# Pooled attention and a max-out feed-forward layer on one core: output weight loaded in two halves, first weight product moved to the prologue, every step reordered

## The chip, the cores and the metric

The kernel runs on one core of a Trainium2 chip. The metric is the device time of one launch in microseconds (us). Three runs of the kernel before gave a median of 227.07 us (225.73 to 227.32). Times inside an execution are counted from the start of the profiled span. For this kernel a difference under about 1% of the time is treated as no change.

## What is computed

For 8 batches of 8 heads, 576 positions and 64 channels, keys and values are averaged over groups of 8 positions, queries attend to the 72 averaged keys, and the result (4608 tokens by 512) passes through three weights, an element-wise maximum and an output weight:

```python
k_p = k.reshape(B, H, Sp, 8, D).mean(axis=3); v_p = v.reshape(B, H, Sp, 8, D).mean(axis=3)
attn = softmax(q @ k_p.T / sqrt(D)); x = (attn @ v_p) as 4608 x 512
h = np.maximum(np.maximum(x @ w1, x @ w2), x @ w3)        # w1..w3: 512 x 768
out = h @ w_out                                           # w_out: 768 x 512
```

## The kernel before, in words

**The work.** The kernel uses the identity h = w1-part + max(0, x(w2-w1), x(w3-w1)). `sub_w` (L392) subtracts w1 from w2 and w3 in place on DVE; `turn_w` (L399) transposes w1, and `linear` (L405) multiplies it with the output weight into `wm` (512x512), 24 matmuls of 512 columns. `hidden` (L439) makes the two products and the maximum for a block of 512 tokens; `project` (L459) adds x times `wm` and h times `w_out` for four groups of 128 tokens. There are nine blocks (0 to 8) of tokens and eight batches (0 to 7) of attention. Blocks 1 to 5 use `out_seven` (L699) for the projection, and blocks 6 to 8 use `seven` (L810) for the hidden part: seven block products in place of eight, with sums of operands prepared on DVE or POOL.

**One batch of attention.** Loads of q, k and v go through POOL's DMA queue and convert float32 to 16 bits (L73, L82, L94). Keys and values are summed over 8 positions by three additions (`fold_steps`, L157) on POOL; only the keys of batches 0 and 1 are summed on DVE (0 with PE), and the values of batch 0 on PE. Queries are turned by PE in batches 0 to 2 (`turn_q`, L188) and by a DMA transpose that SP issues from batch 3 on (step `T`, L350). `scores` (L239) multiplies, ACT takes the exponential, `values` (L301) multiplies with the folded values, DVE normalises, and `turn_x` (L284) turns the result into `xT`: by PE up to batch 2, by SP's DMA transposes after that.

**The order.** Nothing is reordered by a scheduler: every engine does its instructions in the order in which the program names them. Four lists hold it. The prologue (L530 to L571) is written as calls. `block(0, {...})` (L870) runs hidden and project of block 0 with steps of batches 0 and 1 at numbered slots. `MIDDLE` (L953) lists blocks 1 to 5, `ORDER` (L906) the rest. A name such as `2:s0-` is a step of batch 2 (q: turn queries, k: turn keys, K: fold keys on DVE, s: scores, v: values, x: turn the result, T: transpose queries by DMA), `1/h` a hidden product of block 1, `1/6` an output product, `1/b2` a sum of operands, `k3+4` four steps of a fold on POOL, `q4<` a load. A trailing `-` issues PE's part and parks the eviction, `+` issues the oldest parked eviction.

**Queues.** The loads at the start are POOL instructions, in the order L112, L120, L127 to L136: q0 (two DMAs), v0 (two), nine parts of w1, w2, w3 (columns 0-255 of each, then 256-511, then 512-767), the whole of w_out, then k1, q1, v1, q2, k2, v2. Each takes one of eight semaphores, so a ninth DMA waits until the DMA eight before it has landed. k0 comes through SP. SP also issues the stores of the output and the DMA transposes, in program order. A load marked `<` waits for the last hidden matmul issued before it and for the last query transpose (L886 to L891).

**PSUM.** The prologue has a pool `ps0` (three tiles `att` of two banks, two tiles `one`). It is closed at L568, and a pool `psp` (two `att`, one `tr`, three `pw`) serves to the end of `MIDDLE`, a third (`psq`) after it.

Of the kernel before, what the change touches and what calls it, by code (L numbers as in the profile page):

```python
# [10 lines left out]
ALU = mybir.AluOpType  # L11


@with_exitstack
def kernel(
# [18 lines left out]
    C = H * D  # L34
# [17 lines left out]
    ld = ctx.enter_context(tc.tile_pool(name="ld", bufs=2))  # L52
    sb2 = ctx.enter_context(tc.tile_pool(name="sb2", bufs=2))
    sb3 = ctx.enter_context(tc.tile_pool(name="sb3", bufs=3))
# [3 lines left out]
    first = ExitStack()  # L58
    stage.enter_context(first)
    pools = [first.enter_context(tc.tile_pool(name="ps0", bufs=1, space=PSUM))]  # L60
# [21 lines left out]
    def load_v(b, eng, dtype=F16, cuts=(0, H)):  # L82
        if b == 0:
            vts[0] = ld.tile([96, 4096], dtype, name="vt0", tag="vt")[:, 0:3072].rearrange(
                "p (h i d) -> p h i d", h=H, i=6)
            src = v[0].rearrange("h (p i) d -> p h i d", i=6)
            return [eng.dma_start(out=vts[0][:, h:g], in_=src[:, h:g])
                    for h, g in zip(cuts, cuts[1:])][-1]
        vts[b] = ld.tile([Sp, H, POOL, D], dtype, name="vt", tag="vt")
        src = v[b].rearrange("h (sp j) d -> sp h j d", j=POOL)  # L90
        return [eng.dma_start(out=vts[b][:, h:g], in_=src[:, h:g])
                for h, g in zip(cuts, cuts[1:])][-1]
# [13 lines left out]
    def load_w(part):  # L106
        for t, wap in zip(w_sb, (moe_w1, moe_w2, moe_w3)):
            nc.gpsimd.dma_start(  # L108
                out=t[:, :, part],
                in_=wap.rearrange("(kc p) j -> p kc j", p=128)[:, :, part])  # L110
# [9 lines left out]
    load_v(0, nc.gpsimd, cuts=(0, 4, 8))  # L120
    pick = const.tile([96, 6, 128], F16, name="pick", tag="pick")
    nc.gpsimd.memset(pick, 1.0)
    for sign in (1, -1):
        nc.gpsimd.affine_select(
            out=pick, in_=pick, compare_op=ALU.is_ge, fill=0.0, base=7 * (sign < 0),
            pattern=[[sign, 6], [-8 * sign, 128]], channel_multiplier=6 * sign)
    for i in range(3):  # L127
        load_w(slice(256 * i, 256 * i + 256))
    nc.gpsimd.dma_start(
        out=wo_sb, in_=moe_w_out.rearrange("(jc p) c -> p jc c", p=128))  # L130
    load_k(1, nc.gpsimd, F16)
    load_q(1)
    load_v(1, nc.gpsimd)
    load_q(2)
    load_k(2, nc.gpsimd)
    load_v(2, nc.gpsimd)  # L136
# [72 lines left out]
    def turn_k(b):  # L209
        pkt = keys(b, PW if b in KP else SC if len(pools) == 3 else ATT)  # L210
# [13 lines left out]
    def score(b, h, out, tp, i0, i1):  # L224
# [3 lines left out]
        rows = slice(64 * (f % 2), 64 * (f % 2) + 64) if len(pools) == 2 else slice(0, 128)  # L228
# [72 lines left out]
    def values(b, c0):  # L301
        tag = (ATT0, ATT, ("val", 1))[len(pools) - 1]
# [21 lines left out]
    ATT0, ONE = ("att", 3), ("one", 2)  # L324
# [16 lines left out]
    def do(b, steps):  # L341
# [3 lines left out]
        for name in steps.split():  # L345
# [12 lines left out]
            elif name[0] == "s":  # L358
                if i == 0 and name[-1] != "+":
                    new_et(b)  # L360
                if len(pools) == 3:
# [18 lines left out]
            elif name[0] == "w":  # L380
                turn_w(i, nc.scalar.copy if i % 2 else nc.vector.tensor_copy)
# [17 lines left out]
    def turn_w(jc, evac):  # L399
        pwt = psum([128, KCH, 128], F16, name="pwt", tag=TR[0], bufs=TR[1])  # L400
# [4 lines left out]
    def linear():  # L405

        for kc in range(KCH):
            pm = psum([128, C], F32, name="pm", tag="pw", bufs=3)
            for jc in range(JCH):
                nc.tensor.matmul(pm, w1T[:, jc, bass.ts(kc, 128)], wo_sb[:, jc, :],  # L410
                                 start=(jc == 0), stop=(jc == JCH - 1))
                if jc == JCH // 2 - 1:
                    yield
            (nc.scalar.copy if kc % 2 else nc.vector.tensor_copy)(
                out=wm_sb[:, kc, :], in_=pm)
            yield
# [22 lines left out]
    def hidden(n):  # L439
# [13 lines left out]
        if n == 0:  # L453
            yield from linear()
# [4 lines left out]
    def project(n):  # L459
        hT = hTs[n]  # L460
        for mm in range(4):
# [5 lines left out]
            for c in ((slice(0, C // 2), slice(C // 2, C)) if last else (slice(0, C),)):  # L467
                tag = PW if len(pools) < 3 else PA if last else PO
# [20 lines left out]
    wm = psum([128, 1024], F32, name="wm", tag="att", bufs=3)[:, 0:512]  # L489
# [9 lines left out]
    def new_pk0():  # L499
        pk0.append(psum([D, 3, 96], F32, name="pk0", tag=ONE[0], bufs=ONE[1]))  # L500
# [16 lines left out]
    def scores4(h):  # L517
        psc = psum([128, 4, 256], F32, name="psc4", tag="att", bufs=3)
# [4 lines left out]
    def scores2(h):  # L523
        psc = psum([128, 2, 512], F32, name="psc2", tag="att", bufs=3)
# [5 lines left out]
    heat(10)  # L530
    add_k0(0, 2)
    new_pk0()
    sum_k0(0, 0)
    sum_k0(0, 1)
    heat(3)
    add_k0(2, 2)
    new_pk0()
    sum_k0(0, 2)
    sum_k0(1, 3)
    for par in range(2):  # L540
        put_k0(0, par, nc.scalar.copy)
    heat(2)
    add_k0(4, 2)
    sum_k0(1, 4)
    sum_k0(1, 5)
    for par in range(2):
        put_k0(1, par, nc.vector.tensor_copy)
    turn_q(0, 0, 5, nc.vector.tensor_copy, ATT0)
    turn_q(0, 5, 9, nc.scalar.copy, ATT0)
    heat(2)  # L550
    scores4(0)
    turn_q(0, 9, 14, nc.vector.tensor_copy, ATT0)
    turn_q(0, 14, 18, nc.vector.tensor_copy, ATT0)
    pool_v(0, 0, 4, ONE, nc.vector.tensor_copy)
    scores4(4)
    pool_v(0, 4, 8, ONE, nc.vector.tensor_copy)
    scores2(0)
    values(0, CHUNKS[0][0])()
    scores2(2)
    values(0, CHUNKS[1][0])()  # L560
    turn_x(0, 0, 0, xns[0, 0], ONE)
    scores2(4)
    sub_w(0, 0, 1, (1,))
    turn_x(0, 128, 0, xns[0, 128], ONE, nc.vector.tensor_copy)
    sub_w(0, 0, 1, (2,))
    sub_w(0, 1, 2)
    scores2(6)
    first.close()  # L568
    pools.append(stage.enter_context(tc.tile_pool(name="psp", bufs=1, space=PSUM,
                                                  reuse_waits="tile")))  # L570
    turn_w(0, nc.scalar.copy)  # L571

    def block(n, plan, stages):

        for slot, end in enumerate(part for stage in stages for part in stage(n)):
            if end:
                end()
            for b, steps in plan.get(slot, ()):  # L580
                if b < B:
                    do(b, steps)
# [116 lines left out]
    def out_seven(n):  # L699
# [21 lines left out]
        def bank(of, m):  # L721
            if n < LAST:
                if of not in banks:
                    if mid:
                        tag = (TR if of == "A" else PW) if len(pools) < 3 else {
# [84 lines left out]
    def seven(n):  # L810
# [41 lines left out]
        def evict(i, g, p):  # L852
# [11 lines left out]
            elif i in (5, 7) and (12 - i, g) in done:  # L864
# [4 lines left out]
    fold_v(1)  # L869
    block(0, {0: [(0, "v2")], 1: [(0, "v3")], 3: [(0, "x2 x3 w1 v4")], 6: [(0, "x4 d1")], 9: [(0, "w2")], 10: [(0, "d2")], 11: [(0, "w3")], 12: [(0, "w4")], 14: [(0, "w5 z")],  # L870
              15: [(0, "S S")], 17: [(1, "K")], 18: [(0, "S S")], 24: [(1, "q0 k")], 25: [(1, "q1")],
              26: [(1, "s0 q2")], 28: [(1, "s3 Q3")], 30: [(1, "s6")], 31: [(1, "v0")],
              32: [(1, "v1 x0")], 33: [(1, "X1 v2 v3")]}, (hidden, project))
    load_k(3, nc.gpsimd)
    load_v(3, nc.gpsimd)
    load_q(3)
    fold_k(2, nc.gpsimd)
    fold_v(2)


# [178 lines left out]
```

## Time and profile before

The profiled execution has a span of 224.5 us; the median of the timed runs is 227.07 us, 2.6 us more, which lies around the span.

| what | value |
|---|---|
| median of 3 runs (lowest, highest) | 227.07 us (225.73, 227.32) |
| span of the profiled execution | 224.5 us |
| PE busy | 213.0 us, 95%, 1884 matmuls |
| DVE, ACT, POOL busy | 157.9, 123.2, 140.9 us |
| share of the chain that ended last: PE, DMA, POOL, DVE | 69%, 12%, 8%, 6% |
| first matmul; end of the last | 1.53 us; about 220.7 us |

The page gives each engine's busy time. PE is busy nearly throughout, so the question at each stage is how much of PE's time goes to waits, to filler (`heat`, L491) or to a slow start. The view of windows gives busy time per stretch; the timeline of one engine gives its instructions in order, each with the idle time before it and who ended it.

### The profile page before, as it was taken

The numbers are of one execution on the slowest core, as the hardware profiler recorded it, in microseconds if no ns is written. First come the engines' busy times: TensorE is split into PE (matmuls) and PEld (weight loads), VectorE is DVE, ScalarE is ACT, GpSimd is POOL, SyncE is SP. The second block draws the span as 40 slices with busy tenths as digits, with TensorE's granted clock in tenths as the row PEclk, the third lists the DMA queues.
The fourth block names the chain that finished last, engine by engine and source line by source line (L and its number), as shares of the span: only waits on it lengthen the run. The fifth ranks groups of instructions, "written<-read, shape, count | busy, mean of one in ns | idle before, by whom it ended". The sixth has DMA issues, their size and how long they took to land.

```text
span 224.5 us, 4870 instructions
## 1 busy us (share of the span) xinstructions
PE 213.0 (95%) x1884; PEld 147.3 (66%) x1885; DVE 157.9 (70%) x308; ACT 123.2 (55%) x239; POOL 140.9 (63%) x121
## 2 busy tenths in 40 slices
PE   7788999999999999999999999999799999999993
PEld 2477744458659744964685478447589667788882
DVE  3658989037998795885679468629767977878940
ACT  2267524846784577266735845493694445564330
POOL 7974300999957969787685669794292903881020
PEclk9999999999999999999999999999999999999999
DMA  6999999989749799739987998599420645200265
GB/s 167 212 197 196 207 208 207 204 170 226 135 106 190 131 177 248 124 58 212 252 93 157 227 217 140 75 257 157 103 56 19 167 100 110 47 0 3 65 198 161
DMA packets 47303, 33.55 MB, mean 149 GB/s; under 512 B 26992, under 2 KB 42288, under 8 KB 47280
## 3 DMA queue, kind: packets, MB, share of 16 engines
q0 software_dynamic: 16944, 16.98, 47.2%
q1 hardware_dynamic: 29888, 15.87, 31.2%
q10 hardware_dynamic: 448, 0.39, 0.7%
q8 instruction: 15, 0.25, 0.4%
q14 instruction: 8, 0.07, 0.1%
HBM read 34.60 MB, written 9.44 MB: 196 GB/s over the span
## 4 chain that ended last, share of the span: by engine, by line
PE 69%; DMA 12%; POOL 8%; DVE 6%; ACT 2%; issue 1%; POOLq 0%; DVEq 0%; ACTq 0%
PE pw L423 22%; PE oA L769 13%; DMA vt<-in_v_dram 8%; PE oC L769 7%; PE pA L846 6%; DMA mw<-in_moe_w_dram 4%; PE pav L305 4%; PE oB L769 3%; PE psc L229 3%; PE po L475 3%; PE pC L846 3%; POOL half L163 2%; PE po L471 2%; DVE xn L315 1%; POOL mw L108 1%
## 5 line engine op out<-in xcount | busy, mean ns | idle before, releaser
L423 PE MATMUL pw<-xT,mw 128*128 128x512 f16 (+1 forms) x336 | 68.4, 349 | 0.2 <-ACT xT L299 0.2
L423 PEld LDWEIGHTS <-mw 128*128 128x128 f16 x336 | 30.7, 98 | 26.3 <-issue 1.8
L163 POOL TENSOR_TENSOR half<-vt 72x1024 f32<-72x1024 f16 (+1 forms) x12 | 29.1, 2443 | 20.5 <-DMA vt<-in_v_dram 13.2
L431 DVE TENSOR_TENSOR hT<-t,pw 128x512 f16<-128x512 f16 (+1 forms) x42 | 25.4, 608 | 21.4 <-PE pw L423 12.1
L234 ACT ACTIVATE et<-psc 72x512 f16<-72x512 f32 (+2 forms) x66 | 33.9, 571 | 9.0 <-PE psc L229 8.9
L165 POOL TENSOR_TENSOR half<-half 72x1024 f32<-72x1024 f32 (+1 forms) x13 | 28.1, 2165 | 10.4 <-DVE rcp L313 5.2
L429 ACT ACTIVATE t<-pw 128x512 f16<-128x512 f32 (+1 forms) x42 | 22.6, 538 | 17.0 <-PE pw L423 16.5
L315 DVE TENSOR_TENSOR xn<-pav,rcp 128x512 f16<-128x512 f32 x40 | 27.7, 691 | 1.4
L163 POOL TENSOR_TENSOR half<-ktFalse 96x768 f32<-96x768 f16 (+1 forms) x11 | 19.3, 1767 | 3.9 <-issue 3.8
L855 ACT CAST pad<-pA 128x512 f16<-128x512 f32 x27 | 15.1, 586 | 11.6 <-PE pA L846 9.1
L780 ACT COPY osb<-oA 128x512 f32<-128x512 f32 x20 | 11.8, 588 | 17.4 <-PE oA L769 17.2
L769 PEld LDWEIGHTS <-tt 128*128 128x128 f16 x200 | 18.9, 98 | 2.4
L229 PEld LDWEIGHTS <-kz 64*128 64x128 bf16 (+1 forms) x161 | 8.8, 95 | 12.4 <-issue 8.0
L305 PE MATMUL pav<-vp,et 72*128 72x65 f16 x320 | 16.4, 194 | 0.6 <-DVE xn L315 0.2
L305 PEld LDWEIGHTS <-et 72*128 72x128 f16 x320 | 15.0, 98 | 3.0 <-issue 1.3
L313 DVE RECIPROCAL rcp<-pav 128x8 f32<-128x8 f32 x40 | 8.1, 202 | 10.9 <-PE pav L305 10.8
L846 PEld LDWEIGHTS <-sw 128*128 128x128 f16 x144 | 13.8, 97 | 2.7 <-issue 0.2
L826 DVE SCALAR_TENSOR_TENSOR hT<-pad 128x512 f16<-128x512 f16 x18 | 14.0, 784 | 1.1 <-ACT pad L859 0.5
L823 DVE TENSOR_TENSOR pad<-pad,pC 128x512 f16<-128x512 f16 x18 | 12.3, 682 | 3.5 <-PE pC L846 2.7
L229 PE MATMUL psc<-qT,kz 64*128 64x256 bf16 (+5 forms) x138 | 13.2, 263 | 1.0 <-DVE qT L197 0.9
L620 POOL TENSOR_TENSOR pad<-xT 128x256 f16<-128x256 f16 x8 | 5.5, 689 | 13.0 <-DMA xT<-xn 13.0
L769 PEld LDWEIGHTS <-hT 128*128 128x128 f16 x126 | 12.3, 98 | 1.4
(122 smaller groups left out, 400.6 us busy)
## 6 DMA issues: line engine op xcount, KB each, us to landing
out_dram<-osb SPq DMA_DIRECT2D x32, 128.0 KB, 4.3
ktFalse<-in_k_dram POOLq DMA_DIRECT2D x7, 576.0 KB, 8.0
qb<-in_q_dram POOLq DMA_DIRECT2D x7, 576.0 KB, 7.7
vt<-in_v_dram POOLq DMA_DIRECT2D x7, 576.0 KB, 11.9
out_dram<-osb SPq DMA_DIRECT2D x11, 256.0 KB, 6.7
mw<-in_moe_w_dram POOLq DMA_DIRECT2D x9, 256.0 KB, 9.4
ktTrue<-in_k_dram SPq DMA_DIRECT2D x3, 384.0 KB, 5.4
out_dram<-ob SPq DMA_DIRECT2D x8, 128.0 KB, 2.8
```

The lines of the kernel that those rows point to most:

```text
L163: yield e.tensor_tensor(out=f[:, at], in0=t[:, at, 0:4, :], in1=t[:, at, 4:8, :], op=ALU.add)
L165: yield e.tensor_tensor(out=f[:, :, 0:2, :], in0=f[:, :, 0:2, :], in1=f[:, :, 2:4, :], op=ALU.add)
L229: nc.tensor.matmul(out, kz_all[b % 2][f % 2][rows, h, :], qTs[b][rows, n + i0:n + i1, 64 * (h % 2):64 * (h % 2) + 64], start=True, stop=True)
L234: nc.scalar.activation(out=out, in_=in_, func=FT.Exp, scale=1.0 / 64.0)
L305: nc.tensor.matmul(pav[:, h // 4, 65 * (h % 4):65 * (h % 4) + 65], ets[b][:, h, c0:c0 + 128], vp_all[:, b, h, :], start=True, stop=True)
L315: nc.vector.tensor_tensor(out=xn, in0=pv[:, :, :, 0:D], in1=rcp.to_broadcast([128, 2, 4, D]), op=ALU.mult)
L423: mm = nc.tensor.matmul(pw, w_sb[wi][:, kc, bass.ts(jc, 128)], x[:, kc], start=(kc == 0), stop=(kc == KCH - 1))
L429: yield lambda t=t, pw=pw: nc.scalar.activation(out=t, in_=pw, func=FT.Relu)
L431: yield lambda t=t, pw=pw: nc.vector.tensor_tensor(out=hT[:, jc, c0:c1], in0=t, in1=pw, op=ALU.max)
L769: nc.tensor.matmul(p, left, right, stop=(r == 4), skip_group_check=True, start=(i in FIRST and r == 0 and (m == 0 or n == LAST)))
L846: mm = nc.tensor.matmul(p[:, w], a[:, kc, bass.ts(g, 128)], b[:, kc, :], start=(i in FIRST and w + kc == 0), stop=(w + kc == 2), skip_grou ...
L855: nc.scalar.copy(out=kept(i, g), in_=p)
```

## The change

1. Tiles of the SBUF pools `ld`, `sb2`, `sb3` are taken from a class `Ring` that numbers the buffers in turn; the same number of buffers.
2. One PSUM pool `psp` serves the prologue, block 0 and `MIDDLE`: in the prologue two `att` tiles, one `tr`, three `pw` (before: three `att`, two `one`).
3. The order of the first loads is a list. w_out is loaded as two DMAs of 256 columns each (`o0`, `o1`; the weights' parts are `w10` for w1, part 0, and so on; `v1 v0` are heads 4-7 and 0-3 of batch 0; `pick` is POOL's own work of making a constant). q1 is loaded ahead of k1.
4. `linear` becomes four pieces of 12 matmuls with 256 columns (rows half i, columns half c), and with all six `turn_w` is named in the prologue.
5. Prologue and block 0 are names in `MIDDLE` (a leading `.` for the prologue, `0/h` and `0/p` for block 0's hidden and project). The folds of values 1, keys 2 and values 2 on POOL are single steps in the list.
6. Loads marked `<<` (k3, v3, q3) wait for no matmul. All of `MIDDLE` and `ORDER` is in a new order with the same steps.

```diff
-    ld = ctx.enter_context(tc.tile_pool(name="ld", bufs=2))
+    ld = Ring(ctx.enter_context(tc.tile_pool(name="ld", bufs=1)), 2)
...
-    pools = [first.enter_context(tc.tile_pool(name="ps0", bufs=1, space=PSUM))]
+    pools = [Ring(stage.enter_context(tc.tile_pool(name="psp", bufs=1, space=PSUM,
+                                              reuse_waits="tile")))]
...
+    LOADS = """
+        w10 v1 v0 w11 pick w12 w20 o0 w30 w21 o1 w22 w31 w32 Q1 K1 V1 K2 V2 Q2
+    """
...
+    def linear(i, c, tag, evac):
+        pm = psum([128, 2, C // 2], F32, name="pm", tag=tag[0], bufs=tag[1])
+        part = slice(C // 2 * c, C // 2 * c + C // 2)
+        for m in range(2):
             for jc in range(JCH):
-                nc.tensor.matmul(pm, w1T[:, jc, bass.ts(kc, 128)], wo_sb[:, jc, :],
+                nc.tensor.matmul(pm[:, m], w1T[:, jc, bass.ts(2 * i + m, 128)], wo_sb[:, jc, part],
                                  start=(jc == 0), stop=(jc == JCH - 1))
...
+        evac(out=wm_sb[:, 2 * i:2 * i + 2, part], in_=pm)
...
     ORDER = """
-        b1 o1- 2a- b3 o1+ k7- b2 1a- 1b- v62- 1a+ k7+ 2a+ b4 T o6- s70- o6+ o2- s70+ o2+ 6a-
+        k7- o1- 2a- 1a- v62- b1 b3 o1+ 1b- b2 1a+ o6- k7+ s70- o2- s71- 2a+ T vpool 6a- o6+ s70+
...
     MIDDLE = """
-        1/h- q4< k4< 1/h+ 1:x2 1:v4- 1/h- 1/h- v4< 1/h+ 1:v4+ 1/h+ 1/h- 1:x3 1/h- 1/h+ 1/h+
+        .h10 .a0 .n .m0 .a1 .n .m1 .h3 .m3 .a2 .m2 .h2 .ka .m4 .m5 .q0 .kb .Q1 .s0 .h2 .Q2 .s2 .T0
+        .Q3 k3<< .S0 .S4 .v4 .v0 .V0 .T3 .s4 .T5 .T4 .T2 .s6 .V1 .T1 0:v2- .e001 .x0 .X1 .l10 0/h
+        .l00 .e011 0:v3- .e012 0:v2+ .e002 0/h- 0:v3+ 0/h- 0/h+ 0/h+ 0:z .L11 0:x2 0:x3 0:d1 .l01
+        0/h- v1+1 0:v4- 0/h- 0/h+ 0/h- 0/h- 0/h- 0/h+ S 0/h- 0/h- 0/h+ 0/h+ S 0/h+ 0/h- 0/h+ 0:v4+
+        1:q0 0/h+ 0/h+ v1+1 0/h- 0/h- 0:d2 1:q2 0/h+ 0/h+ 0/h- 1:K 0/h+ v1+1 0/h- 0:x4 0/h- 0/h+
+        1:q1 S v1+1 1:k- k2+2 0/h- 0/h+ 0/h+ 0/h- 1:k+ v3<< 0/p 1:s0- 1:s0+ q3<< 0/h+ 1:s0+ 1:s0+
+        k2+1 1:s0+ S 0/p 0/p 1:s3- 1:s3+ 1:s3+ 1:Q3 S 1:s3+ 1:s3+ 0/p 1:s6- 1:s6+ 1:s6+ 0/p 1:v0
+        1:v1 0/p 1:v2- k2+1 v2+1 1:x0 v2+1 S 0/p S 1:X1 0/p 1:v3- 1:v2+ 1/h- 1:v4- 1/h+ 1:x2 1/h-
...
-        4/h+ 4/h- 4/b1 4/h+ 4/h ! k6+2 5:s6- 5:s6+ 4/h 4/h 4/b3 4/b2 4/b4 5:s6+ ! k6+2 4/1-
+        4/7- 5:x0 4/1+ 4/2+ 5:v2- 5:v1+ v6+1 5:x1 v6+1 4/6- 5:v2+ 6:T 4/7+ 5:v3- 6:k- q7< 5:v4-
+        4/6+ 5:x2 4/5- 4/b4 5:v3+ 4/5+ 5/h- 6:k+ 4/3- 4/4- 6:s0- 5:v4+ v7< 5/h- 5/h+ 5/a1 6:s0+
...
-        5/h+ 6:s3- 5/h+ 7:T 6:s3+ 5/h- 6:s3+ 5/h- 6:s3+ 6:s3+ 5/h+ 6:s6- 5/h+ 6:s6+ 6:s6+ 5/h
-        5/h- 6:v0 5/h+ 5/h- 6:x0 6:v1- 5/h+ 6:v1+ 6:x1
+        6:v0- 6:v1- 5/h+ 5/h- 6:v0+ 6:x0 6:v1+ 7:T 5/h+ k7+1 4/3+ 5/h+ 5/h- 5/h- 5/h+ 5/h+ 6:x1
+        k7+1
     """
```

In the prologue's names, `h10` is ten filler matmuls, `a` and `m` the sum of batch 0's keys, `q0 Q1 Q2 Q3` the turning of its queries (through the single tile `tr`), `s` and `S` scores, `v4 v0` the folding of its values by PE, `V` values, `T0` to `T5` the six `turn_w` (`T4 T5` need `w12`, `T2 T3` need `w11`), `l10 l00 L11 l01` the four pieces of `linear` (the second digit is the half of w_out), `e` and `0:d` the subtractions.

More of the change, by code (lines that the diff above doesn't have):

```diff
@@ L119 @@
     make_identity(nc, identh)
[L120 to L136, printed above, removed]
+    loads()
     kz_all = [[const.tile([128, H, 128], BF16, name=f"kz{i}{par}", tag=f"kz{i}{par}")
@@ L550 @@
[L550 to L582, printed above, removed]
+    TAGS = {"q": TR, "t": PW, "l": PW, "v": PW, "x": PW}
@@ L867, in seven @@
         return product
[L869 to L878, printed above, removed]
     folding = {}
@@ L986, in middle @@
                     pieces[n] = hidden(n)
-                parts(name, lambda: next(pieces[n]))
+                parts(name, lambda: next(pieces[n]) or (lambda: None))
+            elif n == 0 and step == "p":
+                if not pieces.get("p"):
+                    pieces["p"] = project(0)
+                next(pieces["p"])
             elif step == "f":
```

224 lines of the change are left out of this document (133 added, 91 removed).

## The prediction

> **What bounds the kernel now.** I read the page's busy times and its 40 slices, then the windows by stage, then PE's and POOL's timelines where PE is not full, and last the query transposes on SP.
>
> ```profile
> PE 213.0 (95%) x1884; PEld 147.3 (66%) x1885; DVE 157.9 (70%) x308; ACT 123.2 (55%) x239; POOL 140.9 (63%) x121
> PE   7788999999999999999999999999799999999993
> DMA  6999999989749799739987998599420645200265
> ```
>
> PE is the bound from about 20 us to 220 us; the loads fill the DMA queue for the first nine slices. So a change of order can gain only where PE waits. The windows say where.
>
> ```profile
> 16.00:32.00 16.00, 15.00 (x148) 10.76 (x149) 13.82 (x36) 9.48 (x20) 5.16 (x7) 1.00 1.32 203
> 32.00:48.00 16.00, 15.77 (x106) 7.55 (x105) 7.55 (x16) 9.22 (x18) 8.53 (x5) 1.00 1.10 201
> 48.00:156.00 108.00, 107.52 (x954) 70.07 (x952) 78.26 (x156) 64.31 (x129) 85.82 (x56) 1.00 0.90 168
> 156.00:182.00 26.00, 23.29 (x245) 19.47 (x243) 21.24 (x39) 15.28 (x29) 14.06 (x12) 1.00 0.47 95
> ```
>
> The first two numbers are the length and PE's busy time: idle 1.0 us, 0.2, 0.5 (of 108) and 2.7. PE's timeline gives the single waits, the idle time in brackets:
>
> ```profile
> 11.12 0.60 PE L229 MATMUL psc<-qT,kz 128*128 128x256 bf16 x4 [0.86 <-DVE qT L197]
> 21.14 0.40 PE L296 MATMUL pxt<-identh,xn 128*128 128x128 f16 x4 [0.40 <-DVE xn L315]
> 47.19 0.42 PE L305 MATMUL pav<-vp,et 72*128 72x65 f16 x8 [0.23 <-POOL vp L167]
> 159.07 0.38 PE L229 MATMUL psf<-qT,kz 128*128 128x320 bf16 x2 [1.49 <-ACT osb L780]
> ```
>
> Between 9.4 and 26 us the matmuls' starts lie 3.7 us further apart than their columns need (handovers between DVE, ACT and PE, and landings). The last line is the largest single wait of the middle; its real cause is in the last fence.
>
> ```profile
> 13.83 0.74 POOL L108 DMA_DIRECT2D mw<-in_moe_w_dram  x1 [0.35 <-DMA vt<-in_v_dram]
> 15.12 0.74 POOL L108 DMA_DIRECT2D mw<-in_moe_w_dram  x1 [0.55 <-DMA mw<-in_moe_w_dram]
> 16.46 0.82 POOL L129 DMA_DIRECT2D mwo<-in_moe_w_out_dram  x1 [0.60 <-DMA mw<-in_moe_w_dram]
> 17.79 0.54 POOL L79 DMA_DIRECT2D ktFalse<-in_k_dram  x1 [0.51 <-DMA mw<-in_moe_w_dram]
> 20.95 0.86 POOL L91 DMA_DIRECT2D vt<-in_v_dram  x1 [1.01 <-DMA mw<-in_moe_w_dram]
> 39.31 4.05 POOL L163 TENSOR_TENSOR half<-vt 72x2048 f32<-72x2048 f16 x1 [13.21 <-DMA vt<-in_v_dram]
> ```
>
> Each load here waits for the one eight before it, so the rows' spacing is the landings' spacing: 1.33 us for a part of a weight (1.38 over all nine). Loads land in the order of issue, one after the other.
>
> ```profile
> L352 SPq DMA_TRANSPOSE qT<-qb x5: 1990/5311/7440, 61.3 to 149.4; - x5
> DMA to landing us min/median/max: 4.0/8.9/10.1
> ```
>
> The last of these five (batch 7) was issued at 149.4, as its queries landed, and took 9.5 us: 158.9. PE went on at 159.07. It, not ACT, ended the 1.49 us.
>
> **The change part by part. Landings.** q0 lands at 10.6 in both. Before: v0 12.1 and 13.5, nine parts to 26.0, w_out 29.8 (3.8 us), k1 32.8, q1 35.5, v1 39.3. After, with the same spacings: w10 12.0, v1 13.4, v0 14.9, w11 16.3, w12 17.7, w20 19.0, o0 21.0, w30 22.4, w21 23.8, o1 25.8, w22 27.1, w31 28.5, w32 29.9, q1 32.6, k1 35.5, v1 39.3. (A half of w_out at the rate of a weight's part, which has the same row length: 1.5 x 1.38 = 2.05; the two cost 0.2 to 0.3 us more than the whole.) What is earlier is w_out; what is later is v0 by 1.4, w20 and w30 by 2.9 and 4.9, and k1 by 2.8. Issues on POOL (0.75 each, `pick` 2.9 in both) stay ahead of the queue.
>
> **Prologue and block 0.** PE takes the new list in order. Its stops: `Q1` until q0's second half (10.6; idle 0.9); `v0` and `V0` for the landing at 14.9 and the copy of 0.42 (1.0); `T5` for w12 (17.7; 0.8); `v2` for s6's exponential (0.25); `l10` for o0 (21.0; 0.85); `L11` for o1 (25.8; 0.55). Between 9.4 and 26 these are 4.4 us against 3.7 before: the linear pieces do not fill waits, they bring their own. DVE's `0:d1` waits for w31 (28.5) and is done at 29.6, before PE's first product that needs it (31.2). PE turns q1 at 32.65, and is at the end of block 0's 14th hidden product at 35.4. There DVE folds k1: 35.5 + 0.95 + 0.55 + 0.35 = 37.4. Behind it on DVE stand that product's maximum (0.69), a sum (0.55), the next maximum (0.69) and four copies of the keys (1.98): 41.3. The 17th product waits for the first of these (0.4), the scores for the last (0.6). From 41.3: scores 0.7 + 0.7 + 0.5, 16 matmuls of project at 0.216 (3.5), the last query turn 0.25, then the exponentials 1.2 before values: 48.2. Before, values began at 47.19 with 6 project matmuls (1.3 us) more behind it: 2.3 us later, of which 0.2 is the wait before 47.19 ceasing to matter later. I take +2.1. Bounds: if all 3.7 us of waits are filled, -3.7; with 0.15 us more at each of ten handovers than I counted, +3.6.
>
> Edits at nothing: 24 matmuls of 512 columns become 48 of 256; rows: ten of 256 in 1.09 us (L769), four of 512 in 0.87 (L423), 0.109 and 0.216, the same per column. The Trainium skill, Perfetto Trace Analysis, Optimizing Tensor Performance, says larger matmuls are more efficient than smaller ones; it gives no price, and these rows do not show it. `Ring` and the single pool: same buffers; two `att` for three makes scores wait for an exponential of 0.75 to 1.0, in the walk above. `k3<<` holds POOL until k1 is folded (37.4); behind it stands v1's fold, which cannot begin before 39.3. If k1 were over 1.9 us later it would push that fold (7.7 us) and PE's values. `v3<<` and `q3<<` put 1.6 us of issue before steps of k2's fold, needed over 5 us later.
>
> **Blocks 1 to 5.** PE idles 0.5 us of 108: the gain is at most 0.5. The loss is where a step stands too close behind its source. The transposes of queries 5 and 6 now stand behind two `xT` transposes on SP (1.2 us each), about 4 us after values begin, and PE has 8.9 us of work from there to their scores (six output products of 1.09, one hidden of 0.86, five values of 0.27, the keys 0.13). At 4.0 to 5 us nothing is lost; at 10.1 it is 5 us each. The next q's load now waits behind them, so little runs beside them: +0.3.
>
> **From 156 us.** The load of q7 moves from the start of block 5's products to before them, so transpose 7 waits for SP instead: values of batch 6, normalise 0.9, one `xT` issue 1.2, so 2.6 us after values; PE reaches its scores 7.0 us after values (0.3, three hidden products 2.6, 4.1 of output and hidden products). Landing after 4.0 to 9.5: idle 0 to 5.1. I take 5 us (issued after most of the loads have landed, nearest to the rows of 4.0 and 4.8): 0.6, a gain of 0.9. The folded keys 7 are wanted at the end of block 5's products, 1.5 us earlier in PE's order; they were done at 154.3 before, and POOL waited 3 to 5 us in every block, which covers it; without that cover it costs 1.5. Of the other 1.2 us idle I take half: -0.5. Sum -1.4, bounds -2.7 and +3.1. After 182 us PE idles only at the very end (last copies and stores): 0.
>
> **Sum.** +2.1 + 0.3 - 1.4 = +1.0 on the 224.5 us span; with 2.6 us around it, 228.1, and 1.0 above the median of 227.07.
>
> **The rivals.**
> Linear fills the waits (the other side). If o0 landed by the time PE reaches `l10` (I have 20.2 against 21.0) and k1 cost nothing, 5.2 us of linear would leave the stretch at 32 and fill 3.7 us of waits: 227.1 - 3.7 = 223.4. For it: PE was full from 32 on. Against: landings decide, and the added bytes ahead of w20 and k1.
> A late transpose. One transpose of queries beside loads takes 9.5 us as before: the term of 156 us becomes +3.1, 232.6. It decides once the transpose takes over 4.4 us. For it: three of five took 8.9 and more. Against: the two without loads beside them took 4.0 and 4.8. The Trainium skill, TensorE: Matmul & The Clock Gate, Part 1, adds that about 3.4 us without PE work halves the clock for as long; here only the first filler matmuls show a slow rate (0.43 us for 0.22), no wait is that long, so this could add an estimated 1.7 us to that case.
> Nothing in the prologue. PE is full either way by 50 us: only the -1.1 from the later stages is left, 226.0.
>
> **How the numbers follow.** The forecast 0.42, linear fills 0.26, a late transpose 0.18, nothing in the prologue 0.14. A difference within 1% (2.3 us) is what a measurement cannot tell from none: faster is the second case with a little of the last, 0.27; slower the third and the upper end of the first (its own range 226 to 230), 0.31; 0.42 between. The range takes half of the second and of the third: 223 to 232.
>
> **What would show it.** Right: w12, o0 and o1 landing at 17.7, 21.0 and 25.8 with PE idle before them, the fold of k1 at 35.5, values of batch 1 at about 48.2, the first hidden product of block 1 near 53 against 51.06, no wait of 1.5 us near 160. Wrong: PE without idle time from 12 to 26 us, or a wait of several us for `qT` before scores 5, 6 or 7.

## The result and the profile after

The changed kernel takes 234.88 us (median of four runs, 232.65 to 235.35), the kernel before 226.40 in the same session (225.14 to 227.32): ratio 1.035 with a 95% interval of 1.029 to 1.041. It is 8.5 us slower; 228.1 was predicted, with 232 as the upper end. The mean granted clock was 1.000 in the run of 232.65 us and 0.985 to 0.993 in the other three, so the slow clock shown below did not come in every run.

The profiled execution has a span of 233.2 us against 224.5. Its page:

```profile
PE 214.8 (92%) x1908; PEld 150.0 (64%) x1909; DVE 169.8 (73%) x311; ACT 121.0 (52%) x236; POOL 142.7 (61%) x125
PE   7687999995999999989999999799999899899993
PEclk9999999998899999999999999999999999999999
PE 54%; DMA 20%; POOL 15%; DVE 7%; issue 2%; ACT 0%; POOLq 0%; DVEq 0%
```

PE's busy time grew by 1.8 us though its work is the same (24 matmuls more, half as wide), and the tenth slice (52 to 58 us) has a hole, with a clock below full speed in it and in the next. In the chain that ended last, DMA went from 12% to 20% and POOL from 8% to 15%. The windows by stage, as before (length, then busy time of PE, PEld, DVE, ACT and POOL, then clock):

```profile
16.00:32.00 16.00, 13.84 (x169) 12.04 (x169) 12.34 (x31) 6.25 (x12) 5.76 (x8) 1.00 1.41 202
32.00:48.00 16.00, 15.63 (x105) 7.78 (x104) 13.39 (x23) 10.18 (x21) 8.56 (x5) 1.00 1.14 207
48.00:156.00 108.00, 102.52 (x900) 66.76 (x900) 79.76 (x145) 59.69 (x122) 81.21 (x56) 0.98 0.86 148
56.00:58.00 2.00, 1.76 (x18) 1.42 (x17) 1.07 (x3) 0.97 (x2) 1.98 (x1) 0.56 1.14 138
58.00:60.00 2.00, 2.00 (x14) 1.49 (x13) 1.28 (x4) 0.38 (x1) 2.00 (x2) 0.59 1.14 240
156.00:182.00 26.00, 25.73 (x253) 19.66 (x252) 20.01 (x39) 16.59 (x32) 14.30 (x8) 1.00 0.71 125
```

From 48 to 156 us PE now idles 5.5 us (0.5 before), and for 4 us its clock is 0.56 to 0.59. From 156 to 182 it idles 0.3 (2.7 before). PE's timeline has the single waits:

```profile
48.11 0.68 PE L328 MATMUL pav<-vp,et 72*128 72x65 f16 x16 [0.21 <-POOL vp L189]
55.47 0.60 PE L440 MATMUL pw<-xT,mw 128*128 128x256 f16 x4 [2.26 <-DVE xT L322]
104.93 1.02 PE L440 MATMUL pw<-xT,mw 128*128 128x512 f16 x4 [0.92 <-DMA xT<-xn]
127.72 0.64 PE L252 MATMUL psc<-qT,kz 64*128 64x320 bf16 x7 [0.47 <-DMA qT<-qb]
147.09 1.02 PE L440 MATMUL pw<-xT,mw 128*128 128x512 f16 x4 [0.96 <-DMA xT<-xn]
186.93 0.49 PE L851 MATMUL pA<-pad,sw 128*128 128x256 f16 x3 [1.18 <-POOL pad L625]
202.41 0.49 PE L851 MATMUL pA<-pad,sw 128*128 128x256 f16 x3 [0.77 <-POOL pad L625]
```

Count as lost what lies between the starts of two matmuls beyond the time of their columns at full clock (0.109 us for 256, 0.216 for 512, other widths on the line through these two). All told 22.0 us are lost against 13.6, which is 8.4 of the 8.7 us between the spans:

| stretch | lost before | lost after | difference | predicted |
|---|---|---|---|---|
| to 50 us | 8.2 | 10.3 | +2.1 | +2.1 |
| 50 to 60 | 0.7 | 4.5 | +3.7 | 0 |
| 60 to 150 | 0.8 | 3.5 | +2.7 | +0.3 |
| after 150 | 4.0 | 3.8 | -0.1 | -1.4 |

The largest wait, 2.26 us before 55.47, is for the copy of x1 (`1:X1`) on DVE. DVE's timeline shows why it was late:

```profile
50.26 1.40 DVE L658 TENSOR_TENSOR so<-so,wm 128x512 f16<-128x512 f16 x1
51.58 3.50 DVE L658 TENSOR_TENSOR so<-wm 128x512 f16<-128x512 f16 x1
55.01 0.41 DVE L322 COPY xT<-pxt 128x512 f16<-128x512 f16 x1
```

Two sums of the output weight (step `S`) stand ahead of the copy, and take 1.40 and 3.50 us; the same form takes 0.42 at 71.85. POOL's timeline at that time is the fold of keys 2, with the two loads `v3<<` and `q3<<` in its middle:

```profile
48.14 3.24 POOL L185 TENSOR_TENSOR half<-ktFalse 96x768 f32<-96x768 f16 x2
51.32 0.87 POOL L97 DMA_DIRECT2D vt<-in_v_dram  x1
52.19 0.77 POOL L105 DMA_DIRECT2D qb<-in_q_dram  x1
52.98 1.81 POOL L187 TENSOR_TENSOR half<-half 96x768 f32<-96x768 f32 x1
```

The first sum ends at 51.66, 0.28 us after the first addition (51.38); the second at 55.08, 0.29 after the second (54.79). So a sum does not run slowly: it stands until POOL's instruction is over. (The second was issued 1.40 us before that addition began, while POOL issued the two loads; the last section comes back to this.) It holds throughout. DVE has 66 sums of weights or operands with both inputs in SBUF (the expectations below say 70). Of these, 14 (4 before) take over 0.15 us longer than their form alone, 13.8 us in all (3.6 before), and every one of them ends 0.28 to 0.30 us (512 columns) or 0.41 to 0.43 (768) after the end of a fold's addition; one more in each kernel, of 0.77 us near the end, ends 0.28 after one of POOL's own sums of operands. DVE's maxima `hT` of block 1 have one input in PSUM; at 58.30 and 59.95, while POOL makes its two additions of 56.02 to 60.21, they take 0.42 as ever. The kernel before showed it too, in two rows of its timelines of DVE and POOL that the prediction passed over:

```profile
59.92 2.57 DVE L653 TENSOR_TENSOR so<-wm 128x512 f16<-128x512 f16 x1
```

```profile
59.53 2.68 POOL L165 TENSOR_TENSOR half<-half 72x1024 f32<-72x1024 f32 x1
```

59.92 + 2.57 is 0.28 after 59.53 + 2.68. There PE waited for nothing behind it. The Trainium skill, SBUF — State Buffer, SBUF: two separate sides, states this: VectorE and GpSimd share a pair of SBUF ports under an exclusive lock, a VectorE instruction with two SBUF inputs contends with a GpSimd instruction that reads SBUF, and whichever starts first holds it for its whole length. These rows agree.

The theory: DVE's two-input sums wait for POOL's folds, and the new order puts them (and what PE needs behind them) beside folds. Rivals: transposes too close behind their source; the work itself being too much for DVE; a slower start alone.

### The profile page after: what moved, and what is told of

Same layout as the page of the kernel before. It is cut to its first block, busy times and chain, and to the rows that moved or that the text cites. A ratio compares the mean times of both kernels' runs of the same rounds, so it can differ in the third digit from the quotient of the medians.

```text
span 233.2 us, 4909 instructions
## 1 busy us (share of the span) xinstructions
PE 214.8 (92%) x1908; PEld 150.0 (64%) x1909; DVE 169.8 (73%) x311; ACT 121.0 (52%) x236; POOL 142.7 (61%) x125
## 4 chain that ended last, share of the span: by engine, by line
PE 54%; DMA 20%; POOL 15%; DVE 7%; issue 2%; ACT 0%; POOLq 0%; DVEq 0%
PE pw L440 23%; PE oA L774 10%; DMA vt<-in_v_dram 7%; DMA xT<-xn 6%; PE oC L774 5%; DMA mw<-in_moe_w_dram 5%; POOL pad L625 4%; POOL half L185 4%; PE pA L851 3%; PE oB L774 3%; PE psc L252 3%; PE pav L328 3%; POOL half L187 2%; DVE so L658 2%; DMA qT<-qb 2%
## 5 line engine op out<-in xcount | busy, mean ns | idle before, releaser
L440 PE MATMUL pw<-xT,mw 128*128 128x512 f16 (+1 forms) x336 | 69.2, 354 | 4.6 <-DVE xT L322 2.3
L440 PEld LDWEIGHTS <-mw 128*128 128x128 f16 x336 | 31.6, 99 | 31.5 <-issue 6.9
L185 POOL TENSOR_TENSOR half<-vt 72x1024 f32<-72x1024 f16 x14 | 30.0, 2160 | 8.3 <-DVE pad L625 5.6
L185 POOL TENSOR_TENSOR half<-ktFalse 96x768 f32<-96x768 f16 x12 | 19.4, 1636 | 5.1 <-issue 4.8
L625 POOL TENSOR_TENSOR pad<-xT 128x256 f16<-128x256 f16 x8 | 6.8, 851 | 15.0 <-DMA xT<-xn 15.0
L831 DVE SCALAR_TENSOR_TENSOR hT<-pad 128x512 f16<-128x512 f16 x18 | 15.2, 851 | 0.6 <-ACT pad L864 0.3
L105 POOL DMA_DIRECT2D qb<-in_q_dram x9 | 7.0, 781 | 12.3 <-PE pqt L217 7.7
L252 PE MATMUL psc<-qT,kz 64*128 64x256 bf16 (+5 forms) x138 | 12.7, 263 | 0.5 <-DMA qT<-qb 0.5
```

The source lines that it names most:

```text
L185: yield e.tensor_tensor(out=f[:, at], in0=t[:, at, 0:4, :], in1=t[:, at, 4:8, :], op=ALU.add)
L252: nc.tensor.matmul(out, kz_all[b % 2][f % 2][rows, h, :], qTs[b][rows, n + i0:n + i1, 64 * (h % 2):64 * (h % 2) + 64], start=True, stop=True)
L440: mm = nc.tensor.matmul(pw, w_sb[wi][:, kc, bass.ts(jc, 128)], x[:, kc], start=(kc == 0), stop=(kc == KCH - 1))
L625: gate[:] = [e.tensor_tensor(out=t[i], in0=a, in1=b, op=ALU.subtract)]
```

## Experiments

In each, the kernel before ran on the same chip (225.9 to 226.6); medians in us, ratios against it with 95% intervals. In the lists, `S` is a sum of the output weight, `f` a sum of hidden weights, `1/a1` a sum of operands of block 1, and `!` lets POOL's next step wait for DVE's latest sum.

**Which half (e1, e2).** e1 has the new prologue and block 0, then the old lists; e2 the old start and the new lists.

```diff
 MIDDLE (e1) = new up to "1:X1 0/p 1:v3- 1:v2+", "1:v3+ v2+1 v2+1", then the old MIDDLE (less 3 of its 4 S); ORDER = old
 MIDDLE (e2) = new from "1/h- 1:v4-" on, with one S each behind 2:q1, 2:q2, 1/a1; ORDER = new
```

> The changed kernel up to the first hidden product of block 1 (its prologue, its block 0, seven of the eight sums of the output weights, its loads), then the steps of blocks 1 to 8 in the order of the kernel before. Stages theory (from the lost PE time of the two traces, after against before: +2.1 us up to 50 us, +3.7 from 50 to 60, +2.7 from 60 to 150, -0.2 later): the first two stay, so 5.8 us above the kernel before, about 232. Rival, the loss is made mainly by query and result transposes that stand late in the new middle: then only the 2 us of the prologue stay, about 228.5.

Measured 232.02, ratio 1.025 [1.019, 1.030]. The wait before 55.5 (2.24 us) and the slow clock are there; behind them little more is lost than before (0.6 us by the same count).

> The kernel before up to the end of block 0, then the new order for blocks 1 to 8 (three of the output weights' sums, which the new order has earlier, are put at query turns and the first sum of operands of block 1). Stages theory: +2.7 us of waits for result and query transposes and about nothing in the last part, about 229. Rival, everything is lost before 60 us: no change, 226.4. A gain over the kernel before would say that the new rest is the better one.

Measured 237.60, 1.051 [1.048, 1.055]: a miss by 8 us. The new rest shifted against the old start put 17 sums under folds: PE waited 1.89 us for the copies of keys behind one, then 2.42 and 1.77 for others. So the halves do not add; what counts is how DVE and POOL lie to each other.

**The stage at 50 us (e3 to e7).** e3 moves the two sums by some 7 us:

```diff
-1:x0 v2+1 S 0/p S 1:X1
+1:x0 v2+1 0/p 1:X1          (and S behind 2:q0 and behind 2:k-)
```

> The changed kernel with only the last two sums of the output weights on DVE moved from before the eviction of x1 of batch 1 to some 10 us later, when POOL has nothing to fold. Port theory (DVE's sums take 1.40 and 3.50 us beside POOL's folds, hold that eviction until 55.0, PE waits 2.26 us, and its clock then falls to 0.56): the wait goes, the clock stays at 1.00, 3.5 to 4.5 us less than the changed kernel, about 231. Rival, DVE is late there for another reason (the values or their normalisation): under 1 us less.

Measured 232.47, 1.027 [1.023, 1.032]. x1 was copied at 51.6 and PE went on at 52.95, but the sums met the fold of values 2 (1.35 and 2.01 us) ahead of the copies of the keys: PE waited 1.18 and 0.70 there, with the clock at 0.65 and 0.50 behind it.

e4 leaves the sums and lets POOL wait for them with the folds:

```diff
-1:k- k2+2 ... k2+1 1:s0+ ... k2+1 v2+1 1:x0 v2+1 S 0/p S 1:X1
+1:k- ... 1:s0+ ... 1:x0 S 0/p S 1:X1 ! k2+2 k2+1 k2+1 v2+1 v2+1
```

> The changed kernel with the sums where they are, but POOL's fold of keys 2 and the first steps of values 2 stand behind the last of these sums. Port theory: the same two sums take 0.35 to 0.6 us each, the eviction of x1 comes at about 51.8, PE waits under 0.4 us and the clock stays at 1.00; 3 to 4.5 us less than the changed kernel, if keys 2, now folded some 4 us later, are not waited for. Rival, the sums are slow by themselves: their rows stay at 1.4 and 3.5 us and the time stays within 1 us.

Measured 237.26, 1.050 [1.047, 1.052]. DVE's timeline has the two sums at their place again:

```profile
50.13 0.41 DVE L658 TENSOR_TENSOR so<-so,wm 128x512 f16<-128x512 f16 x1
50.46 0.42 DVE L658 TENSOR_TENSOR so<-wm 128x512 f16<-128x512 f16 x1
```

They took 0.41 and 0.42 us and the wait was gone, so POOL it is. But the fold of keys 3 came earlier (at 69.30; 73.82 in the changed kernel), and two sums of operands met it (4.39 and 2.15 us): PE waited 3.48 us before 75.09.

e5 puts the sums, and the first operand sum, where POOL does nothing:

```diff
-1:x0 v2+1 S 0/p S 1:X1 ... 1/a1 2:s3- v4< 2:s0+ 1/h+ 1/h- 1/h+ 2:s3+ f
+1:x0 v2+1 0/p 1:X1 ... 2:s3- v4< 2:s0+ 1/h+ 1/h- 1/h+ 1/a1 S 2:s3+ S f
```

> Sums on an idle port (my theory): the two sums of the output weight and the first sum of block 1's inputs stand where GpSimd folds nothing. Each then takes 0.41 to 0.44 us, x1 is evicted by 51.7, the first hidden product of block 1 starts near 53.0 with no wait before it, the granted clock stays at 1.00 up to 100 us, and the time is the changed kernel's less the 2.3 us wait and the 1.7 us at a slow clock: about 230.9. Late transposes (rival: what lies behind 100 us is the loss, and 50 to 60 us was its own accident): as much, since it makes the same of this stage; the two part after it. Too much work for VectorE (rival): the two sums cost their place wherever they stand, so PE waits some 2 us somewhere from 60 to 75 us and the time stays near 232.5, as with the sums moved a little.

Measured 231.27, 1.022 [1.017, 1.028]: 3.6 less than the changed kernel. DVE's timeline:

```profile
52.11 0.42 DVE L322 COPY xT<-pxt 128x512 f16<-128x512 f16 x1 [1.35 <-PE pxt L319]
64.81 0.42 DVE L658 TENSOR_TENSOR so<-so,wm 128x512 f16<-128x512 f16 x1
65.14 0.42 DVE L658 TENSOR_TENSOR so<-wm 128x512 f16<-128x512 f16 x1
```

Now the copy waits for PE, not PE for the copy. The clock is 1.00 throughout this stage, and the loss from 50 to 60 us is 0.1. Too much work for DVE is out.

e6 fills the wait with ten matmuls that nothing reads:

```diff
-1:v3- 1:v2+ 1/h-
+1:v3- 1:v2+ .f10 1/h-       (f: ten matmuls of 512 columns into a tile of pw)
```

> Ten matmuls of 512 columns whose result nothing reads are put ahead of block 1's first hidden product, where PE stands idle for 2.3 us; all else is the changed kernel. Clock theory (the wait of 2.3 us lets the granted clock fall to 0.56, and PE loses some 1.7 us after it): the eviction of x1 stays late (55.0), the fillers end before 55.5, the clock reads 1.00 from 56 to 60 us, and the time is 1.7 less, 233.2. Rival (the clock falls for another reason, such as how much the other engines draw, or the matmuls are slow for want of operands): the matmuls after 55.5 still take 0.43 us for 512 columns and the time stays at 234.9.

Measured 232.01, 1.025 [1.020, 1.031], 2.9 less. The copy was as late (55.18). Its windows:

```profile
56.00:58.00 2.00, 1.75 (x25) 1.48 (x23) 1.56 (x4) 0.97 (x2) 1.92 (x2) 1.00 1.16 136
58.00:60.00 2.00, 2.00 (x24) 1.84 (x23) 1.59 (x5) 1.46 (x4) 2.00 (x2) 1.00 1.09 205
```

So the slow clock came from the wait: 2 us at 0.56 and 2 at 0.59 cost an estimated 1.7 us. Smaller waits further on shrank too (0.47 became 0.16 near 127, the 0.77 near 202 is gone); why is not shown.

e7 gives only the copy of x1 to ACT (`1:X1` becomes `1:x1`).

> Only the copy of x1 from PSUM goes to ScalarE; the sums stay beside the folds. Theory (the copy waits behind the slow sums on VectorE; PE waits for nothing else there): x1 is evicted near 52.3, PE's first hidden product of block 1 starts near 53.0, no wait of over 0.5 us up to 58, and the time falls by 3 to 4 us, to about 231.4. Rival (VectorE is late with the normalised outputs too, and PE waits for those or for the hidden activations instead): the wait moves to 55 to 58 us and the time falls by less than 2 us, 233 or more.

Measured 234.07 (231.56 to 235.06), ratio 1.032 [1.025, 1.039] without the slowest run: the rival. PE's first hidden product started at 52.90, and PE then waited 2.32 us before 55.82 for the normalised values, the next thing behind the same two sums.

**All folds (e12, e13).** Both kernels with POOL's folds of batches 2 to 7 cut, so that the keys and values of these batches are not computed:

```diff
+d = slice(0, 1) if short else slice(0, D)          # first two additions: 1 of 64 elements
-yield e.tensor_tensor(out=out, in0=f[:, :, 0, :], in1=f[:, :, 1, :], op=ALU.add)
+yield e.memset(out, 0.01) if short else ...
```

> The kernel before, with GpSimd's folds of batches 2 to 7 cut: the first two additions of each take one of 64 elements, the last is a memset of the whole result. So the pooled keys and values of those batches are not computed; the loads, VectorE, ScalarE and TensorE do what they did. Theory (folds hold VectorE's two-input sums): only 4 of 70 sums were held before, 3.6 us in all, and PE waited for none of them, so little is gained there; GpSimd being done sooner may bring loads forward. 226.0, within 1.5 either way. Rival (the folds cost nothing to the other engines): the same 226.

> The changed kernel with the same cut (the pooled keys and values of batches 2 to 7 are not computed). Theory (GpSimd's folds hold VectorE's sums: 14 of 70 held, 13.8 us, in the changed kernel): no sum at 50 us is held, no sum after it either; the wait before 55.5 is gone, the clock stays at 1.00, and the waits near 104, 127 and 146 us fall to 0.3 or less in sum from 2.3. Left over is the start: some 2.3 us above the run of the kernel before with the same cut: about 228.3, so 6.5 below the changed kernel. Rival (transposes that stand too close behind their values cause the waits from 100 to 150): the 3.6 us of the sums are gained and the waits from 100 to 150 stay at about 2.3: 230.8 to 231.3.

Measured 226.03 (1.002 [0.999, 1.004]) and 236.51 (1.047 [1.045, 1.050]). No sum was held by a fold behind 50 us in either. In the changed kernel the wait before 55.5 and the slow clock behind it are gone, as the theory had it. Near 127 and 147 us waits stay (0.32, now for a sum on DVE, and 0.94 for a transpose of x), and no sum is held there. And a new one ate the gain:

```profile
104.11 1.87 PE L448 MATMUL pw<-xT,mw 128*128 128x512 f16 x4 [4.45 <-DMA xT<-xn]
```

With its folds short, POOL issued the loads of q5 and k6 at 93.86 and 94.64, 5.4 us sooner than in e5. The transposes of x issued at 93.94 and 95.84 then took 6.77 and 8.13 us; the one issued at 92.58, ahead of the loads, took 2.42. The 4.45 us cost the clock as well (0.50 from 104 to 110 us). So POOL's slowness seems to have kept these loads out of the way; that is read from the order of the rows, and no run moved these loads alone.

**The waits from 100 to 150 us (e10, e15, e18).** All on e5. e10 names the loads `q5<` and `k6<` later, behind `2/4-`:

> The changed kernel with the sums on an idle port (231.27), and the loads of q5 and k6 issued at the end of block 2's products instead of within them. In that run the third transpose of x, issued at 97.77, took 3.74 us beside these two loads (issued 99.30 and 100.09), where the two before it took 2.4, and PE waited 0.94 us for it. Theory (the loads slow it): it takes 2.4 to 2.6 us, the wait falls under 0.2, the time to 230.4, if the later loads cost nothing. Rival (the values' step stands too close ahead of the products whatever the queue does): the transpose takes the same 3.7 us or the wait stays over 0.6, and the time stays at 231.3.

Measured 230.99, 1.021 [1.017, 1.025]; it tells nothing, since POOL issued the loads at the same place (98.50 and 99.29): in POOL's own order they still stand between the same two additions. The transpose took 3.82 us.

e15 moves a sum of hidden weights that was held (1.42 us for 0.55) ahead of the normalising that the transpose needs:

```diff
-3:x0 3:v1+ f 2/6- ... 2/3+ v6< f 3/h+
+3:x0 3:v1+ 2/6- ... 2/3+ v6< f f 3/h+
```

> The changed kernel with the sums of the output weight on an idle port (231.27), and one more sum moved: a sum of two hidden weights, which in that run took 1.42 us at 94.88 beside a fold (0.55 alone) ahead of the normalising of the values whose transpose PE waits for at 101.65. It goes to where the next such sum stands, some 12 us later. Theory (the held sum makes the transpose late): the normalised values are ready 1.4 us earlier, the transpose is issued near 96.4 instead of 97.8, the wait of 0.94 us falls under 0.2, and the time to 230.4, if the sum is not held elsewhere. Rival (the transpose is slow or its step too close whatever VectorE does): it lands as late against PE's products, the wait stays over 0.6, and the time stays at 231.3.

Measured 229.77, 1.018 [1.015, 1.022], 1.5 less than e5; the wait of 0.94 is gone. So that wait too was a held sum.

e18 is e15 with one output product moved ahead of block 5's first hidden product, where 1.08 us were left:

```diff
-4/5+ 5/h- 6:k+ 4/3- 4/4-
+4/5+ 4/3- 6:k+ 5/h- 4/4-
```

> The run with the sums of the output weight on an idle port and one hidden-weight sum moved (229.77), with one output product of block 4 (1.09 us of TensorE) ahead of block 5's first hidden product instead of behind it. There that hidden product waited 1.08 us at 141.96 for a transpose issued at 138.74 and landed at 141.82. Theory (the step stands too close behind its values; nothing is held there): the transpose lands as before, PE has work until then, the wait falls under 0.2, and the time to 228.8. Rival (what PE wants next is as late): the wait moves to the next step (the scores of batch 6 or the next hidden product) and the time stays within 0.3 of 229.8.

Measured 229.38 (229.06 to 229.77; e15 had 229.57 to 230.80), 1.013 [1.010, 1.016]. In between, and hardly to be told from e15: the wait for the transpose is gone, but the moved product waits 0.67 for ACT to empty its PSUM bank.

**The start (e17, e11, e16).** e17 is e1 with the two sums where the old list has its own, at 68 us.

> The changed kernel's prologue and block 0, and the old order of everything behind it; the two sums of the output weight that were held at 50 us stand at 68 us instead, where the old order has its own. Theory (the start costs 2.1, the held sums and the clock 3.6, and the rest of the first such run is the old kernel's): no wait before block 1's first hidden product (near 53.0), the clock at 1.00, and 228.2, 2.1 above the kernel before. Rival (the shifted start puts the old order's sums and folds out of step further on): held sums with PE waiting after 60 us, and 229 or more.

Measured 227.48 (one run of nine, of 253.33 us, is not in the ratio), 1.008 [1.004, 1.011]: 4.5 less than e1, from two sums moved. What the new start costs by itself is 0.9 to 2.5 us.

e11 and e16 put `linear` and the loads `o0 o1` back (on e5), e16 with the first sums behind the late loads and all copies on ACT:

```diff
-w20 o0 w30 w21 o1 w22 w31 w32 Q1 ... .X1 .l10 0/h .l00 ... .L11 ... .l01
+w20 w30 w21 w22 w31 w32 o0 o1 Q1 ... 1:q0 0/h+ 0/h+ .l10 .l00 .L11 .l01
```

> The changed kernel with the sums on an idle port (231.27), with one part of the change undone: the product of the first with the output weight goes back behind block 0's first hidden products, its two loads behind all nine parts of the three weights, and one more step of project goes ahead of the values of batch 1. Prediction's sum (the linear pieces bring their own waits, 1.3 us for o0 and 0.3 for o1; they fill none): PE's waits from 16 to 30 us fall by 1.4 us, the wait for q1 at 33 is covered; but the values of batch 1 cannot start before GpSimd's fold of v1 ends (48.0), so at most 1.0 us of it reaches the end: 230.3. Rival (the linear pieces did fill waits that are there anyway): PE waits as much for the weights' parts in their place, and the time is 231.3 or more.

> The changed kernel with the sums on an idle port (231.27), and the product of the first with the output weight put back behind block 0's first hidden products, its two loads behind the nine parts of the weights. Unlike the first try, the first two sums of the output weight stand behind the landing of its second half (29.9), and all four copies of the product are ScalarE's, so that VectorE has nothing in front of the fold of k1 at 35.5. Prediction's sum (the linear pieces bring waits of 1.1 to 1.5 us of their own, and fill none): PE's waits from 16 to 30 us fall by 1.2, and as the values of batch 1 cannot start before the fold of v1 ends (48.0), at most 1.0 reaches the end: 230.3. Rival (linear pieces fill waits): waits for the weights' parts in their place, 231.3 or more.

Measured 241.90 (1.074 [1.067, 1.081]) and 242.47 (1.074 [1.070, 1.078]): both missed, for a reason that neither theory had. PE ran dry for 2.9 us by 32 us, and DVE came to the fold of k1 only at 40, just as POOL took up v1. DVE and POOL in e16:

```profile
42.20 4.64 DVE L189 TENSOR_TENSOR kp<-halfh 96x384 bf16<-96x384 f16 x1
```

```profile
42.43 4.19 POOL L185 TENSOR_TENSOR half<-vt 72x1024 f32<-72x1024 f16 x2
```

An addition of 0.35 us took 4.64, to 0.23 us behind POOL's; PE waited 2.53 us for the keys. Whether the linear pieces in the prologue pay stays open.

**The wait at 159 us of the kernel before (e8, e9, e14).** The load `q7<` stands earlier on POOL: ahead of the fold of values 6 (e8), ahead of the last part of keys 6 (e9), or between the halves of the first addition of values 6 (e14).

```diff
 (e8)  4/1- q7< v6+2 5:v0       (e9)  5:s6+ q7< ! k6+2 4/1-      (e14) 4/1- v6+1 q7< v6+1 5:v0
```

> The kernel before, with nothing changed but the load of batch 7's queries, put ahead of the fold of batch 6's values on GpSimd's queue (issued near 137 instead of 142). My reading of the 1.49 us wait before 159.07 (it is the transpose of batch 7's queries, late because its load is late): the load lands near 145, the transpose is issued then and lands by 155, the wait is gone, and the time is 224.7 against 226.0. Rival (the earlier load runs beside the transposes of batch 5's inputs and of batch 6's queries and slows those, so PE waits there instead): no gain, 226 or a little more. Rival (the wait belongs to ScalarE's copy, as the profile names it): the wait stays and the time is 226.0.

Measured 226.98, 1.003 [1.001, 1.006]. Moving the load pushed the fold's first addition by 2.3 us (it ends at 143.68 for 141.42), onto a sum: 0.42 became 2.43 us, and PE waited 0.58 before 145.41 and 0.70 before 159.09.

> The kernel before with the load of batch 7's queries put into the stretch in which GpSimd waits for VectorE (132.4 to 134.3 us), so that no fold behind it moves. In the run with this load 4 us earlier the folds moved too, and a sum of VectorE took 2.43 us beside one (0.42 before). Theory (that collision ate the gain): all sums stay under 0.6 us at 140 to 145, the keys of batch 7 are folded by 154.5, the transpose lands by 154, the wait near 159 falls to 0.2 or less, and the time is 225.2. Rival (the transposes of batch 5's inputs are slowed by the load beside them): PE waits near 138 to 140 for them, and the time stays at 226.4. Rival (another wait, for the copies of batch 7's keys on ScalarE, stands at 158 anyway): the wait is 0.7 and the time 225.8.

Measured 236.14 (230.53 to 241.43 in six runs); the ratio, of the two fastest alone, is 1.025 [1.018, 1.033]. The load waits for the transpose of batch 6's queries (L886 to L891), whose landing at 140.55 it cannot pass; in e9 it stood on POOL until 141.12 ahead of keys 6, and PE waited 5.43 us for those.

> The kernel before with the load of batch 7's queries issued between the two halves of the first addition of batch 6's values (near 139.3 instead of 142.2; sooner it cannot be, since it waits for the transpose of batch 6's queries, landed at 138.1). So the fold behind it is 0.8 us later, not 1.5, and the sum of VectorE at 141.7 is held for some 0.8 us instead of 2.0. Theory: no wait of PE near 145, the transpose of batch 7's queries lands by 156, the wait near 159 falls from 1.49 to 0.5 or less, and the time is 225.2 against 226.1. Rival (the wait near 159 belongs to what comes next, the keys of batch 7 and their copies): it stays at 0.7 or more and the time is 226 or more.

Measured 225.54, 0.9985 [0.9968, 1.0003]. The sum took 0.83, and the wait fell from 1.49 to 0.82, now for ACT's copies of batch 7's keys. It is the fastest version seen, and not to be told from the kernel before.

## Why the prediction was wrong

**Landings and start: right.** Measured (predicted): w12 17.3 (17.7), o0 21.2 (21.0), o1 25.9 (25.8), q1 33.0 (32.6), k1 35.8 (35.5), v1 39.7 (39.3). PE waited for w12 0.43 (0.8), o0 1.12 (0.85), o1 0.31 (0.55); values of batch 1 began at 48.11 (48.2). The rival that linear fills the waits is out: the pieces did bring their own. That the total agrees to 0.1 us is in part luck. By the count of the table, 1.2 us more were lost from 9.4 to 26 us where 0.7 were forecast, and 0.7 from 26 to 50 where the rest of the +2.1, 1.4, was. And the values were released, after 0.21 us of waiting, by POOL's fold of v1, which ended at 48.06; the forecast had it begin at 39.3 and take 7.7, so end near 47.0.

**The step that failed: "first hidden of block 1 near 53".** Its matmuls started at 55.47; without a sum ahead of the copy they started at 52.95 (e3). DVE's order around it was never walked: only in the fold of k1 were sums priced, at 0.55 each, and the two ahead of x1's copy had no term. Nor had the sums a second price, beside a fold, although the row of 2.57 us was in the trace of before. They were priced at their time alone. The step that "`v3<<` and `q3<<` put 1.6 us of issue before steps of k2's fold, needed over 5 us later" failed with it: they stand between the fold's first addition and its second, which ended at 54.79, and the second sum stood until then (read from the rows; no run moved these loads alone). In place of nothing, the two sums cost 3.6 us (e5).

**"No wait is that long".** The rival of the late transpose set the clock aside with this. The Trainium skill, TensorE: Matmul & The Clock Gate, Part 1, puts the halving at about 3.4 us of idleness; here 2.26 us sufficed in the profiled run, and 1.18 and 0.70 within 3 us in e3, while single waits of 1.49 (before) and 1.43 (e17) left it at 1.00. The measurement decides: an estimated 1.7 us of the 3.6 is the clock.

**Blocks 1 to 5: +0.3 against +2.7.** The walk looked at the query transposes alone. They cost 0.47 ("at 4.0 to 5 us nothing is lost"; it took 4.0). The transposes of x had no term: one was late by a held sum (0.92; shown by e15), one stands close behind its values (0.96; e18 removed that wait and met another). The remaining 0.3 or so was not tested.

**From 156 us: -1.4 against -0.1.** The transpose of batch 7's queries took 4.2 us (5 predicted), and its scores, at 166.47, did not wait for it: right. From 156 to 182 us PE idles 0.3 in place of 2.7. But "after 182 us PE idles only at the very end" failed: the new order has POOL's sums of x begin at 182.06 with PE at their heels (1.18 and 0.77 us). Two of the sums in front of the 1.18 took 1.00 and 1.11 us (from 182.81 and 183.76; 0.67 alone), beside two of DVE's maxima with two inputs in SBUF that took 0.91 and 1.15 (from 182.36 and 183.20; 0.69 alone): there DVE and POOL seem to hold each other in turn. All this is read from the trace; no run tested it.

**Around the span.** The forecast put 2.6 us around the span. Each run on record has 1.7 to 1.9 (234.93 for a span of 233.2), so +1.0 on 224.5 gives some 227.3 and not 228.1; the forecast of no change is the same.

**The rival on the slower side** was a late query transpose, which took 3.9 to 4.2 us for batches 5 to 7 and decided nothing. Slower came by a mechanism that no rival had.

## What to carry to other kernels

Before an order is changed, list for every DVE instruction with two SBUF inputs what POOL runs beside it, and price it at the rest of POOL's instruction; then ask what PE needs next in DVE's queue. Read the longest single row of a group, not only the usual one. Moving one load or one sum shifts POOL against DVE for the rest of the kernel, so the halves of two orders cannot be priced apart.

## What was not expected of the hardware

- A two-input sum can stand for more than one POOL instruction: it was issued at 51.58 with two loads being issued on POOL, and ended behind the addition that followed; in e4 at 68.57 the same, behind two additions (4.39 us). The issue of loads alone does not do it: the sums at 71.85, 72.18 and 72.65 in the changed kernel, beside three loads being issued, took 0.42, 0.55 and 0.55. Why these two missed their turn stays open.
- The other way round the price is smaller: in e15 POOL's two additions that began 0.07 us after such a sum (0.55 us from 138.88) took 4.53 us for 4.20, and POOL's short sums behind 182 us took up to 1.11 for 0.67.
- With two loads issued at the same time, DMA transposes took 6.8 and 8.1 us, where the one ahead of the loads took 2.4 (e13); the kernel with the short folds is 1.6 us slower than the changed one. That the loads are the cause is read from the rows, not tested.
